# Gated two-branch decode attention: both A heads of a set scored by row on VectorE, one softmax merge per set, and a re-dealt indirect DMA

## The chip, the core and the metric

The kernel runs on one core of one Trainium2 chip. The metric is the device time of the program in microseconds (us), lower is better. Five engines matter: TensorE (PE, with its weight loads PEld), VectorE (DVE), ScalarE (ACT), GpSimd (POOL) and the sync queue (SP) that issues nearly all DMAs. "Span" is the time from the first to the last instruction in the profiled execution.

## The reference

Two attention blocks answer one query token (x, 448 numbers) from caches of 8192 keys, and a sigmoid gate mixes them. Block A has 16 heads with a cache of its own each; block B has 16 query heads that share 8 caches in pairs. Head size is 256, all in fp32.

```python
def _A_ref(x, k_cache, v_cache, wq, wo):          # H, Dh = 16, 256
    q = (x @ wq).reshape(B, Sq, H, Dh).transpose(0, 2, 1, 3)
    scores = jnp.einsum("bhqd,bhkd->bhqk", q, k_cache) * (Dh ** -0.5)
    p = _softmax(scores, axis=-1)
    o = jnp.einsum("bhqk,bhkd->bhqd", p, v_cache)
    return o.transpose(0, 2, 1, 3).reshape(B, Sq, H * Dh) @ wo
...                                               # _B_ref: the same, k and v repeated for pairs of heads
x = A_x
g = _sigmoid((x * gate_w).sum(-1, keepdims=True))
return g * a + (1 - g) * b
```

The key caches and the query weights of both blocks are multiplied by 64 when the inputs are made, so the softmax is sharp.

## The kernel before, in words

**The stream.** All inputs (caches, query weights `wq`, output weights `wo`) are laid out by the host in the order of use in one array, `stream`. SP copies it through a ring of three slots, each 128 partitions by 15872 floats; one DMA fills one slot but at the end, where the last slots come in several pieces. A slot's next DMA is issued when every instruction that reads the slot is done. `plan()` (L220) cuts the stream into these fills and nothing else sets the order of the work: the program walks through the fills, and the pieces in each, and issues for each piece what can be done with it (`piece`, L625).

**Sets and tiles.** The work goes in 8 sets. A set has one B cache (two query heads, unit 2), then two A heads (units 0 and 1; `UNITS`, L199, gives the order 2, 0, 1). A unit is cut into 4 tiles of 2048 keys: a K tile and a V tile of 4096 floats per partition each. V tiles follow their K tiles with a lead of three (`LEAD`): after K tile i comes V tile i-3. A set's `wo` comes in behind the fourth tile of the next set, and the next set's `wq` behind the eighth. I number K and V tiles 0 to 95 through the whole stream; set 7 has tiles 84 to 87 (B), 88 to 91 (first A head, A0) and 92 to 95 (second A head, A1).

**Two ways to score a K tile.** `scores` (L454) has the keys turned (256 numbers of a key down the partitions): PE multiplies them with the query in 8 matmuls into PSUM (`sc`), DVE takes the minimum of the negated scores (`mn`, `st`), ACT exponentiates (`px`), and DVE transposes the 128x512 result (`pr`) into weights for PE. `scores_by_row` (L481) has one key per row: DVE multiplies the whole tile in place by the query laid over all partitions (`slot<-slot,qa`, 4096 elements per partition), sums each key's 256 products (`sr<-slot`), takes the minimum over a partition and over 32 partitions (`mn`, `mt`, `st`), ACT exponentiates 16 numbers (`pxr`), and DVE spreads them over the columns that PE wants (`pr<-pxr,cols`). Where a tile is cut by the end of a slot, multiply and sum run once for each part. `BY_ROW` (L200) says which units go by row; before, that is unit 0 of each set (A0), and the host lays out the keys to suit.

**After the scores.** `attend` (L509) multiplies a V tile with `pr` on PE in 8 matmuls and accumulates in PSUM (`o`); after a unit's fourth V tile `take` (L521) folds the two halves (ACT, then DVE) into `ob`. Each tile has its own minimum and sum; `gather` (L529) puts them in `gs`, and `combine` (L543) merges them for one unit on one partition: a matmul with ones, a minimum (`mnr`), exponentials (`ew`, ACT), products and a sum (`es`, `z`), a reciprocal, and weights times the gate (`wr`). `column` (L567) turns these into a column (`sel`) by a matmul, `project_o` (L577) applies it to `ob`, and `emit_set`/`emit` multiply with `wo` into `Y`. These steps are put off by `wait` and `tick` (L615, L618): a tick comes at the end of every K tile, and of the last three V tiles. The order of instructions on each engine is the order in which the program issues them, and each engine takes its own in that order.

**Query and side DMA.** `project` makes a set's queries on PE from `wq`; `spread` (L436) lays them out for both ways of scoring. For set 4 part of `wq` comes by an indirect DMA that POOL issues, from an array `side` into the front of fill 23's slot, in a choice of partitions (`SIDE_SHARE`, L208) that gives some of the 16 DMA engines more rows than others; the rest (`ws`) comes in the stream.

**The end.** The last V tile comes in three pieces and set 7's `wo` in four; then `project_o` for the last unit, four `emit` calls, a copy of `Y` (`ys`) and the DMA out.

Of the kernel before, what the change touches and what calls it, by code (L numbers as in the profile page):

```python
# [10 lines left out]
P = 128  # L11
# [188 lines left out]
BY_ROW = {(s, 0) for s in range(NS)}  # L200
# [7 lines left out]
SIDE_SHARE = {0: 8, 2: 8, 7: 8, 8: 8, 15: 8, 4: 7, 1: 5, 3: 1, 6: 1, 10: 1}  # L208
# [3 lines left out]
SB, SA = 2 * DH, 64  # L212
# [54 lines left out]
def gated_decode_attention_kernel(  # L267
# [23 lines left out]
    zero = const.tile([P, P], BF16, name="zero")  # L291
    nc.vector.memset(zero, 0.0)

    POS, CAP = {}, {}
    for M in (2, 1):
        r = R[M]
        POS[M] = const.tile([P, NG, r], F32, name=f"pos{M}")
        nc.gpsimd.iota(POS[M], pattern=[[BLK + r, NG], [1, r]], base=0, channel_multiplier=-1,
                       allow_small_or_imprecise_dtypes=True)
        nc.vector.tensor_scalar(POS[M], POS[M], 0.0, None, op0=OP.is_equal)  # L300
        mask = const.tile([P, NT], F32, name=f"mask{M}")
        nc.vector.tensor_reduce(mask, POS[M].rearrange("p g (t m) -> p t g m", m=M), axis=AX.XY, op=OP.add)

        CAP[M] = const.tile([P, NT], F32, name=f"cap{M}")
        nc.vector.tensor_scalar(CAP[M], mask, 3.0e38, OFF, op0=OP.mult, op1=OP.add)
# [15 lines left out]
    rows4 = const.tile([P, 4], F32, name="rows4")  # L321
# [6 lines left out]
    in4 = const.tile([P, 2, NG], F32, name="in4")  # L328
    nc.vector.tensor_copy(in4[:, 0, :], rows4)
# [6 lines left out]
    cols = const.tile([P, NT, NG, NT], F32, name="cols")  # L336
    nc.vector.memset(cols, 0.0)
    for t in range(NT):
        nc.vector.tensor_copy(cols[:, t, :, t], in4[:, 1, :])

    spread32 = const.tile([2 * BLK, P], F32, name="spread32")
    nc.vector.memset(spread32, 0.0)
    nc.vector.memset(spread32[BLK:BLK + 1, :], 1.0)

    QB = {}
    for par in range(2):
        for r in (r for r in range(3) if (par, r) not in BY_ROW or (par + 2, r) not in BY_ROW):
            QB[par, r] = const.tile([P, 2, 64], F32, name=f"qb{par}{r}")
            nc.vector.memset(QB[par, r], 0.0)

    xz = const.tile([P, KF + 2, BLK], F32, name="xz")
    nc.vector.memset(xz, 0.0)
# [15 lines left out]
    gate = const.tile([1, 2], F32, name="gate")  # L370

    def clear(t, n):
        nc.tensor.matmul(t[:, :n], zero, zero[:, None, :n // 4].to_broadcast([P, 4, n // 4]), start=True, stop=False, skip_group_check=True)
# [10 lines left out]
    def prepare(gw):  # L384
        clear(YY[0], D)
        gp = ps_s.tile([1, 1], F32, name="sm")
        for c in range(KF + 1):
            nc.tensor.matmul(gp, xz[:, c, 0:1], gw[:, c:c + 1], start=(c == 0), stop=(c == KF))
# [3 lines left out]
        nc.vector.reciprocal(gate[:, 0:1], ge)  # L392
        nc.vector.tensor_scalar(gate[:, 1:2], gate[:, 0:1], -1.0, 1.0, op0=OP.mult, op1=OP.add)
# [5 lines left out]
    def project(s, c0, w):  # L399

        if c0 == 0:
            QR[s] = ps_s.tile([2 * BLK, 2 * DH], F32, name="sm")
        q = QR[s]
        for j in range(w.shape[1]):
            a, c = divmod(c0 + j, KF)
            for a in (a,) if a < 2 else (0, 1):
                c = c if c0 + j < 2 * KF else KF
                nc.tensor.matmul(q[BLK * a:BLK * (a + 1), :], xz[:, c if c < KF else KF + a, :], w[:, j, :],
                                 start=(c == 0), stop=(c == KF), skip_group_check=True)
        if c0 + w.shape[1] == 2 * KF + 1:  # L410
            copy_out(s, q)
# [5 lines left out]
    def project_side(s, view, far):  # L417
# [4 lines left out]
        for a in range(2):  # L422
            nc.tensor.matmul(q[BLK * a:BLK * (a + 1), :], xz[:, KF + a, :], rest, start=True, stop=False,
                             skip_group_check=True)
# [11 lines left out]
    def spread(s):  # L436
# [7 lines left out]
        for r, a, h, M in ((2, 0, 0, 2), (0, 1, 0, 1), (1, 1, 1, 1)):  # L444
            if (s, r) in BY_ROW:
                qa = ps_s.tile([P, DH], F32, name="sm")
                nc.tensor.matmul(qa, spread32, qr[:, h * DH:(h + 1) * DH], start=True, stop=True)
                QA[s, r] = small.tile([P, DH], F32, name="qa", bufs=1)
                nc.scalar.activation(QA[s, r], qa, AF.Copy, scale=-scale)
                continue  # L450
            nc.vector.tensor_scalar(QB[s % 2, r][:, :, BLK:BLK + M], qt[:, h:h + M, :, a].rearrange("p h e -> p e h"),
                                    -scale, None, op0=OP.mult)

    def scores(u, t, j0, kt):  # L454
# [6 lines left out]
        qb = QB[u[0] % 2, u[1]]  # L461
# [10 lines left out]
        nc.vector.tensor_tensor(st[:, 0, t:t + 1], mn, CAP[M][:, t:t + 1], op=OP.min)  # L472
        px = small.tile([P, NB * BLK], F32, name="px")
        nc.scalar.activation(px, sc, AF.Exp, bias=st[:, 0, t:t + 1], scale=-1.0, accum_out=st[:, 1, t:t + 1])
        pr = small.tile([P, NB * BLK], F32, name="pr", bufs=LEAD + 2)
# [5 lines left out]
    def scores_by_row(u, t, j0, kt):  # L481
# [10 lines left out]
        if j0 + n < ROWS:  # L492
# [9 lines left out]
        pr = small.tile([P, NB * BLK], F32, name="pr", bufs=LEAD + 2)[:, :ROWS * NG * NT].rearrange(  # L502
            "p (q c k) -> p q c k", c=NG * NT, k=2)
# [25 lines left out]
    def gather(u):  # L529

        M = heads(u)
        GS[u] = small.tile([P, 2, NG, NT, M], F32, name=f"gs{M}")
        st = ST[u][:, :, None, :].to_broadcast([P, 2, NG, NT])
        if u in BY_ROW:
            nc.vector.tensor_tensor(GS[u][:, :, :, :, 0], st, in4[:, :, :, None].to_broadcast([P, 2, NG, NT]), op=OP.mult)
        elif M == 1:
            nc.vector.tensor_tensor(GS[u][:, :, :, :, 0], st, POS[M][:, None].to_broadcast([P, 2, NG, NT]), op=OP.mult)
        else:
            pos = POS[M].rearrange("p g (t m) -> p g t m", m=M)
            for k in range(2):  # L540
                nc.vector.tensor_tensor(GS[u][:, k], ST[u][:, k, None, :, None].to_broadcast([P, NG, NT, M]), pos, op=OP.mult)

    def combine(u):  # L543

        M = heads(u)
        n = NG * NT
        gi = 1 if u[1] == 2 else 0
        T = ps_s.tile([1, 2, n * M], F32, name="sm")
        nc.tensor.matmul(T, ones, GS[u].rearrange("p k g t m -> p k (g t m)"), start=True, stop=True)
        mn = small.tile([1, 2], F32, name="mnr")  # L550
        z = small.tile([1, 2], F32, name="z")
        ew = small.tile([1, 2 * n], F32, name="ew")[:, :n * M]
        es = small.tile([1, 2 * n], F32, name="es")[:, :n * M]
        nc.vector.tensor_reduce(mn[:, :M], T[:, 0, :].rearrange("p (c m) -> p m c", m=M), axis=AX.X, op=OP.min)
        for m in range(M):
            nc.scalar.activation(ew[:, m::M], T[:, 0, m::M], AF.Exp, bias=mn[:, m:m + 1], scale=-1.0)
# [232 lines left out]
```

## Time and profile before

| what | value |
|---|---|
| time, median of 3 runs (lowest to highest) | 1005.79 us (1005.64 to 1006.03) |
| time of the profiled execution | 1005.72 us |
| its span | 1004.1 us |
| bytes moved, mean rate over the span | 432.51 MB, 431 GB/s |
| DMA queue of the stream, share of 16 engines' time | 99.3% |
| instructions on PE / PEld / DVE / ACT / POOL | 3176 / 3176 / 650 / 307 / 20 |
| ACT busy | 94.0 us (9%) |

All instructions carry the line of one helper that records them (L150), so groups are told apart by their tiles, written out<-in. A view by groups gives: engine, operation, tiles, shape, count, then busy us, mean ns of one, and the idle time before them. A view in order of time gives: start in us from the span's start, length, engine, what, count, and in brackets the idle time of the engine before it with what ended that. PE needs two MATMUL records for each matmul of fp32 data (16 records are one tile's 8 matmuls).

### The profile page before, as it was taken

Reading aid. Unit: us, or ns where it says so; the run is one execution under the profiler, and the core shown is the slowest. Engines: PE = TensorE matmul, PEld = TensorE weight load, DVE = VectorE, ACT = ScalarE, POOL = GpSimd, SP = SyncE. Lnnn points to the kernel's source line nnn. Section 1 sums busy time; section 2 is a strip of 40 time slices with the busy share of each in tenths; the row PEclk is TensorE's granted clock in tenths of the full one; section 3 lists DMA queues with packets and bytes.
Section 4 is the critical chain, followed back from the end, with each engine's and each line's share of the span. In section 5 each row is a group of like instructions: output and inputs, shape, how many; then the busy total and the mean of one; then the engine's idle time right before and its main releaser. Section 6 shows DMA issues by size and latency. Waiting matters only on the chain.

```text
span 1004.1 us, 7447 instructions
## 1 busy us (share of the span) xinstructions
PE 586.9 (58%) x3176; PEld 172.7 (17%) x3176; DVE 459.2 (46%) x650; ACT 94.0 (9%) x307; POOL 4.4 (0%) x20
## 2 busy tenths in 40 slices
PE   0845745565754655656837566445755646656466
PEld 0211211121211111112212121111211112111112
DVE  2386223961248521467213951248521585215852
ACT  0100110010100110001100011100110001100101
POOL 1000000000000000000000000000000000000000
PEclk9977777767777887777777777877777767977779
DMA  9999999999999999999999999999999999999998
GB/s 405 441 432 420 443 441 416 438 441 435 426 428 445 433 436 425 437 432 433 436 435 426 440 436 428 431 440 435 428 433 436 434 437 426 431 440 441 423 421 366
DMA packets 9257, 432.51 MB, mean 431 GB/s; under 512 B 1105, under 2 KB 1233, under 8 KB 1873
## 3 DMA queue, kind: packets, MB, share of 16 engines
q1 hardware_dynamic: 9080, 431.14, 99.3%
q0 software_dynamic: 144, 0.89, 0.2%
q8 instruction: 25, 0.41, 0.1%
q14 instruction: 8, 0.07, 0.0%
HBM read 433.20 MB, written 0.00 MB: 431 GB/s over the span
## 4 chain that ended last, share of the span: by engine, by line
DMA 71%; PE 14%; DVE 13%; ACT 1%; issue 0%; SPq 0%
DMA slot<-in_stream_dram 71%; PE o L150 7%; DVE sr L150 5%; DVE slot L150 5%; PE sc L150 5%; PE sm L150 2%; DVE pr L150 1%; DVE mn L150 1%; ACT px L150 1%; ACT pxr L150 0%; DVE st L150 0%; ACT ew L150 0%; DVE mt L150 0%; DVE ob L150 0%; DVE es L150 0%
## 5 line engine op out<-in xcount | busy, mean ns | idle before, releaser
L150 PE MATMUL o<-slot,pr 128*32 128x512 f32 (+1 forms) x1536 | 345.4, 756 | 206.7 <-DMA slot<-in_stream_dram 206.7
L150 PE MATMUL sc<-slot,qb 128*32 128x512 f32 x1024 | 195.3, 725 | 111.2 <-DMA slot<-in_stream_dram 111.0
L150 DVE TENSOR_REDUCE mn<-sc 128x1 f32<-128x512 f32 x64 | 44.2, 690 | 326.6 <-PE sc L150 291.2
L150 DVE TENSOR_TENSOR slot<-slot,qa 128x4096 f32<-128x4096 f32 (+6 forms) x39 | 142.4, 3652 | 45.0 <-DMA slot<-in_stream_dram 45.0
L150 PEld LDWEIGHTS o<-slot,pr 128*32 128x32 f32 (+1 forms) x1536 | 80.3, 143 | 385.7 <-DMA slot<-in_stream_dram 231.2
L150 DVE TENSOR_REDUCE sr<-slot 128x16 f32<-128x4096 f32 (+6 forms) x39 | 142.5, 3654 | 1.3
L150 PEld LDWEIGHTS sc<-slot,qb 128*32 128x32 f32 x1024 | 45.7, 130 | 227.5 <-DMA slot<-in_stream_dram 127.1
L150 ACT ACTIVATE px<-sc,st 128x512 f32<-128x512 f32 x64 | 44.0, 687 | 395.6 <-DVE st L150 395.6
L150 DVE STREAM_TRANSPOSE pr<-px 128x512 f32<-128x512 f32 x64 | 45.6, 713 | 54.1 <-ACT px L150 54.1
L150 PE MATMUL sm<-slot,xz 128*32 128x512 f32 (+2 forms) x130 | 46.2, 694 | 32.9 <-DVE xz L150 22.7
L150 ACT ACTIVATE pxr<-sr,st 128x16 f32<-128x16 f32 x32 | 9.8, 308 | 377.0 <-DVE st L150 377.0
L150 PE MATMUL sm<-sel,ob 128*128 128x1 f32 (+1 forms) x96 | 18.2, 294 | 33.9 <-DVE ob L150 33.9
L150 DVE SCALAR_TENSOR_TENSOR ob<-o,half,ob 128x256 f32<-128x256 f32 x24 | 11.4, 473 | 49.6 <-ACT ob L150 49.5
L150 PEld LDWEIGHTS sm<-sel,ob 128*128 128x128 f32 x96 | 16.2, 237 | 58.7 <-DVE ob L150 51.0
L150 PEld LDWEIGHTS sm<-slot,xz 128*32 128x32 f32 (+1 forms) x130 | 11.3, 131 | 65.3 <-issue 29.7
L150 DVE TENSOR_TENSOR pr<-pxr,cols 128x256 f32<-128x256 f32 x32 | 13.6, 426 | 15.0 <-ACT pxr L150 15.0
L150 PE MATMUL Y<-slot,ocs 128*1 128x448 f32 (+1 forms) x176 | 17.0, 450 | 4.7 <-DMA slot<-in_stream_dram 4.6
L150 ACT ACTIVATE ob<-o,half 128x256 f32<-128x256 f32 x24 | 11.3, 469 | 47.4 <-PE o L150 47.2
L150 PE MATMUL sm<-px,spread 64*128 64x256 f32 x16 | 7.6, 568 | 13.1 <-DVE es L150 13.1
L150 PE MATMUL sm<-ones,wr 1*128 1x1 f32 x48 | 9.9, 273 | 8.3 <-DVE wr L150 8.2
L150 PEld LDWEIGHTS sm<-ones,wr 1*128 1x128 f32 x48 | 7.8, 203 | 30.4 <-DVE wr L150 15.5
L150 ACT ACTIVATION_READ_ACCUMULATOR px<-sc,st 128x1 f32 x64 | 12.3, 193 | 0.0
(69 smaller groups left out, 150.0 us busy)
## 6 DMA issues: line engine op xcount, KB each, us to landing
slot<-in_stream_dram SPq DMA_DIRECT2D x47, 7936.0 KB, 41.9
slot<-in_stream_dram SPq DMA_DIRECT2D x1, 7944.0 KB, 21.7
slot<-in_stream_dram SPq DMA_DIRECT2D x1, 7840.0 KB, 46.8
slot<-in_stream_dram SPq DMA_DIRECT2D x1, 7776.0 KB, 48.6
slot<-in_stream_dram SPq DMA_DIRECT2D x1, 5792.0 KB, 42.2
slot<-in_stream_dram SPq DMA_DIRECT2D x1, 5376.0 KB, 34.9
slot<-in_stream_dram SPq DMA_DIRECT2D x2, 2048.0 KB, 33.4
slot<-in_stream_dram SPq DMA_DIRECT2D x1, 2816.0 KB, 31.1
```

The source lines that it names most:

```text
L150: ins = getattr(engine, method)(*args, **kw)
```

## The change

It has six parts.

1. `BY_ROW` now holds units 0 and 1 of every set: A1 is scored by row too. `in_order` lays out its keys to suit. `spread` makes one 128x512 tile `qa` for both A heads (one matmul, one ACT copy) where it made one of 128x256 for A0 and a scaled copy `qb` for A1. `pr` of the A tiles becomes a tile of its own, `prr`, with 8 buffers; the B tiles' `pr` has 4.
2. `combine` and `column` run once for a set, after the last K tile of A1, for all four heads: `gather` puts all in one `gs`; the products go on DVE (B) and ACT (A). `project_o` of the set's first two units moves behind that `column`.
3. The indirect DMA goes into 64 partitions (before 55) with 6 pieces of 704 floats each (before 7 of 576); `ws` has 1472 floats per partition (before 1856). The fills of the stream are the same but for that one piece.
4. The two matmuls of the last `wq` piece become one of 64 columns.
5. The gate is a DVE product, a DVE sum and one matmul, where it was four matmuls; `gate` has four entries.
6. Constants: the masks for one head alone and `spread32` go, zeroed tiles are joined in one (`empty`), `zero` shrinks, `ys` uses a scratch buffer.

The core of the diff:

```diff
-BY_ROW = {(s, 0) for s in range(NS)}
+BY_ROW = {(s, r) for s in range(NS) for r in (0, 1)}
...
-SIDE_SHARE = {0: 8, 2: 8, 7: 8, 8: 8, 15: 8, 4: 7, 1: 5, 3: 1, 6: 1, 10: 1}
+SIDE_SHARE = {0: 8, 2: 8, 7: 8, 8: 8, 15: 8, 4: 6, 1: 5, 5: 3, 13: 3, 14: 3, 6: 2, 10: 1, 3: 1}
...
-SB, SA = 2 * DH, 64
+SB, SA = 2 * DH, 192
...
     def spread(s):
...
-        for r, a, h, M in ((2, 0, 0, 2), (0, 1, 0, 1), (1, 1, 1, 1)):
-            if (s, r) in BY_ROW:
-                qa = ps_s.tile([P, DH], F32, name="sm")
-                nc.tensor.matmul(qa, spread32, qr[:, h * DH:(h + 1) * DH], start=True, stop=True)
-                QA[s, r] = small.tile([P, DH], F32, name="qa", bufs=1)
-                nc.scalar.activation(QA[s, r], qa, AF.Copy, scale=-scale)
-                continue
-            nc.vector.tensor_scalar(QB[s % 2, r][:, :, BLK:BLK + M], qt[:, h:h + M, :, a].rearrange("p h e -> p e h"),
-                                    -scale, None, op0=OP.mult)
+        nc.vector.tensor_scalar(QB[s % 2][:, :, BLK:BLK + 2], qt[:, :, :, 0].rearrange("p h e -> p e h"),
+                                -scale, None, op0=OP.mult)
+        qa = ps_s.tile([P, 2 * DH], F32, name="sm")
+        nc.tensor.matmul(qa, rows4[:2 * BLK, 1:2].to_broadcast([2 * BLK, P]), qr, start=True, stop=True)
+        both = small.tile([P, 2 * DH], F32, name="qa")
+        nc.scalar.activation(both, qa, AF.Copy, scale=-scale)
+        for r in range(2):
+            QA[s, r] = both[:, r * DH:(r + 1) * DH]
...
-    def combine(u):
...
-        for m in range(M):
-            nc.scalar.activation(ew[:, m::M], T[:, 0, m::M], AF.Exp, bias=mn[:, m:m + 1], scale=-1.0)
...
+    def combine(s):
...
+        nc.vector.tensor_reduce(mn, T[:, 0], axis=AX.X, op=OP.min)
+        nc.vector.tensor_tensor(ew, T[:, 0], mn[:, :, None].to_broadcast([1, NG, n]), op=OP.subtract)
+        nc.scalar.activation(ew, ew, AF.Exp, scale=-1.0)
+        nc.vector.tensor_tensor(es, ew, T[:, 1], op=OP.mult)
+        nc.vector.tensor_reduce(z, es, axis=AX.X, op=OP.add)
+        nc.vector.reciprocal(z, z)
+        nc.vector.tensor_tensor(z, z, gate, op=OP.mult)
...
+        for h in range(NG):
+            if h < 2:
...
+                nc.vector.tensor_scalar(w, ew[:, None, h, :, None].to_broadcast([1, 2, n, 2]), z[:, h:h + 1], None,
+                                        op0=OP.mult)
+            else:
...
+                nc.scalar.activation(w, ew[:, None, h, :, None].to_broadcast([1, NG, n, 2]), AF.Copy, scale=z[:, h:h + 1])
...
             if t == NT - 1:
                 gather(u)
-                wait(1, combine, u)
-                wait(2, column, u)
+                if u[1] == UNITS[-1]:
+                    s = u[0]
+                    wait(1, combine, s)
+                    wait(2, column, s)
+                    for r in UNITS[:2]:
+                        wait(2 if s == NS - 1 else 3, project_o, (s, r))
...
-                    if u != TILES[-1][0]:
+                    if u[1] == UNITS[-1] and u[0] < NS - 1:
                         wait(1, project_o, u)
```

**DVE at the last K tile (tile 95).** `sc` is the scores in PSUM, `slot_50` and `slot_51` two slots of the ring, `sr` the row sums. Before:

```order
L150 TENSOR_REDUCE mn_84<-sc 128x1
L150 TENSOR_TENSOR st_82<-mn_84,cap_11_59 128x1
L150 STREAM_TRANSPOSE pr_85<-px_61 128x8x2x32
L150 TENSOR_TENSOR gs_81_121<-st_82,pos_9_57 128x32
L150 TENSOR_REDUCE mnr_99<-sm 1x1
```

Now, at the same place:

```order
L150 TENSOR_TENSOR slot_50<-slot_50,qa_68 128x2560
L150 TENSOR_REDUCE sr_84<-slot_50 128x10
L150 TENSOR_TENSOR slot_51<-slot_51,qa_68 128x1536
L150 TENSOR_REDUCE sr_84<-slot_51 128x6
L150 TENSOR_REDUCE mn_77<-sr_84 128x1
L150 STREAM_TRANSPOSE mt_86<-mn_77 128x32
L150 TENSOR_REDUCE st_75<-mt_86 128x1
L150 TENSOR_TENSOR prr_96<-pxr_88,empty_63 128x256
L150 TENSOR_TENSOR gs_82<-st_75,in_13_61 128x2x16
L150 TENSOR_REDUCE mnr_102<-sm 1x4
```

Three small instructions per tile are replaced by a multiply and a sum over the whole tile, in two parts here, and four small ones.

**PE at the end of the stream.** `o<-slot` are the matmuls of V tiles 92 to 95, `sm<-gs` is combine's matmul, `sm<-ones,wr` (now `sm<-ones,px`) column's, `sm<-sel,ob` project_o's. Before:

```order
L150 MATMUL sm<-sel_110,ob_114 128x1 x2
L150 MATMUL o<-slot_51,pr_87 32x512 x8
L150 MATMUL o<-slot_51,pr_88 32x512 x8
L150 MATMUL sm<-gs_81_121,ones_49 1x32
L150 MATMUL o<-slot_51,pr_89 32x512 x8
L150 MATMUL sm<-ones_49,wr_109 128x1
L150 MATMUL o<-slot_52,pr_85 32x512 x8
L150 MATMUL sm<-sel_111,ob_115 128x1 x2
```

Now:

```order
L150 MATMUL o<-slot_51,prr_93 32x512 x8
L150 MATMUL o<-slot_51,prr_94 32x512 x8
L150 MATMUL sm<-gs_82,ones_49 1x128
L150 MATMUL o<-slot_51,prr_95 32x512 x8
L150 MATMUL sm<-ones_49,px_58 128x1 x3
L150 MATMUL sm<-sel_108,ob_98 128x2 x2
L150 MATMUL sm<-sel_108,ob_99 128x1 x2
L150 MATMUL o<-slot_52,prr_96 32x512 x8
L150 MATMUL sm<-sel_108,ob_100 128x1 x2
```

combine's and column's matmuls keep their places among the V tiles; the project_o of the set's first two units (`ob_98`, `ob_99`) now stands between column and the last V tile's matmuls.

More of the change, by code (lines that the diff above doesn't have):

```diff
@@ L567, in column @@
[L567 to L575 removed]
+        T = ps_s.tile([1, 2, NG, n], F32, name="sm")
+        nc.tensor.matmul(T, ones, GS.pop(s).rearrange("p k h g t -> p (k h g t)"), start=True, stop=True)
```

150 lines of the change are left out of this document (65 added, 85 removed).

## The prediction

> **What bounds the kernel now.** First the page: the engines' busy time, the slices, and the issues.
>
> ```profile
> PE 586.9 (58%) x3176; PEld 172.7 (17%) x3176; DVE 459.2 (46%) x650; ACT 94.0 (9%) x307; POOL 4.4 (0%) x20
> ...
> DMA  9999999999999999999999999999999999999998
> ...
> slot<-in_stream_dram SPq DMA_DIRECT2D x47, 7936.0 KB, 41.9
> ```
>
> The DMA engines are busy in every slice; DVE in less than half of the span. A fill lands 41.9 us after its issue (median), and moving it takes 7936 KB / 431 GB/s = 18.9 us, so fills are queued some 23 us ahead. The stream sets the time as long as slots come free early enough and little is left to do when the last byte lands. The chain that ended last, in order of time, shows how little that is before:
>
> ```profile
> 965.10 35.92 DMA slot<-in_stream_dram
> 1001.06 0.99 PE Y L150 x32
> 1002.07 0.28 DVE ys L150
> ```
>
> All of the last 36 us is waiting for the stream; behind it come the last output matmuls, a copy and the DMA out. The change puts no byte less into the stream worth naming, so the questions are two: does DVE still free the slots in time, and when is it done with the last K tile?
>
> **What a K tile costs DVE, by either way.** The groups of instructions, shapes apart:
>
> ```profile
> L150 DVE TENSOR_REDUCE sr<-slot 128x16 f32<-128x4096 f32 x25 | 110.5, 4420 | 0.9
> L150 DVE TENSOR_TENSOR slot<-slot,qa 128x4096 f32<-128x4096 f32 x25 | 110.4, 4418 | 26.6 <-DMA slot<-in_stream_dram 26.6
> L150 DVE STREAM_TRANSPOSE pr<-px 128x512 f32<-128x512 f32 x64 | 45.6, 713 | 54.1 <-ACT px L150 54.1
> L150 DVE TENSOR_REDUCE mn<-sc 128x1 f32<-128x512 f32 x64 | 44.2, 690 | 326.6 <-PE sc L150 291.2 <-PE sm L150 35.3
> ```
>
> By row it is 4.42 + 4.42 us and small steps; by PE's scores 0.69 + 0.71 and small steps. The four A0 tiles of set 7 and one A1 tile, in DVE's order of time:
>
> ```profile
> 919.69 4.43 DVE L150 TENSOR_TENSOR slot<-slot,qa 128x4096 f32<-128x4096 f32 x1 [8.60 <-DMA slot<-in_stream_dram]
> ...
> 942.51 4.42 DVE L150 TENSOR_TENSOR slot<-slot,qa 128x4096 f32<-128x4096 f32 x1
> 946.96 4.42 DVE L150 TENSOR_REDUCE sr<-slot 128x16 f32<-128x4096 f32 x1
> ...
> 952.88 0.48 DVE L150 SCALAR_TENSOR_TENSOR ob<-o,half,ob 128x256 f32<-128x256 f32 x1
> 953.28 3.88 DVE L150 TENSOR_TENSOR slot<-slot,qa 128x3584 f32<-128x3584 f32 x1
> ...
> 963.88 0.18 DVE L150 TENSOR_TENSOR gs<-st,in 128x32 f32<-128x32 f32 x1
> 963.98 0.69 DVE L150 TENSOR_REDUCE mn<-sc 128x1 f32<-128x512 f32 x1
> ...
> 979.61 0.69 DVE L150 TENSOR_REDUCE mn<-sc 128x1 f32<-128x512 f32 x1 [9.31 <-PE sc L150]
> ...
> 981.34 0.71 DVE L150 STREAM_TRANSPOSE pr<-px 128x512 f32<-128x512 f32 x1 [0.84 <-ACT px L150]
> ```
>
> A whole tile by row takes DVE from 942.51 to 952.88, 10.37 us; one that is cut takes from 953.28 to 963.88, 10.60; `ob` adds 0.40 and `gs` 0.10. A tile by PE's scores takes it from 979.61 to 982.05, 2.4, with a wait for ACT in it. DVE is not idle between these tiles: the first waited for its fill, and all later ones for DVE itself.
>
> **The stream's pace, and whether slots come free.** PE's rows at 938.42, 957.19 and 975.90 show when fills 49, 50 and the second part of 51 landed:
>
> ```profile
> 938.42 9.20 PE L150 MATMUL o<-slot,pr 128*64 128x512 f32 x32 [5.88 <-DMA slot<-in_stream_dram]
> 953.42 1.01 PE L150 MATMUL sm<-sel,ob 128*128 128x2 f32 x4 [5.80 <-DVE ob L150]
> 957.19 3.64 PE L150 MATMUL o<-slot,pr 128*32 128x512 f32 x16 [2.76 <-DMA slot<-in_stream_dram]
> 975.90 1.08 PE L150 MATMUL sc<-slot,qb 128*32 128x512 f32 x4 [5.92 <-DMA slot<-in_stream_dram]
> ```
>
> A fill of 15872 floats per partition each 18.7 us, so one K and one V tile (8192 floats) each 9.7 us: less than the 10.4 us that DVE needs. Eight by-row tiles take DVE 8 x 10.4 = 83 us; the stream needs 8 x 9.7 = 77.3 us for them and twice 4.2 us for the 3584 floats of `wo` and of `wq` that lie between, 85.8 in all. So within a set DVE falls back by some us at a time, not without end, and in the four B tiles (39 us of stream, 2.4 us of DVE each) it catches up. A fill holds at most some 2 by-row tiles, 21 us of DVE; 2 us more than a fill's 18.7; with up to 5 us carried over from the fills before, a slot is free at most about 26 us after it landed. Its next DMA is due when the two fills behind it have landed, 37.4 us after: over 10 us remain. I count nothing for slots. If the cover went, each us beyond it would be a us of idle DMA, seven times over (rival 1).
>
> **The last set, step by step.** Fill 48 brings tiles 88 and 89, and DVE starts at 919.69, as before: by the argument above it has caught up, and the fill's contents and place are unchanged. From here to the end DVE has eight by-row tiles in a row and always more landed than it can eat: five whole (88, 89, 90, 92, 94), three cut by a slot's end (91, 93, 95), two `ob`, one `gs` between. 5 x 10.37 + 3 x 10.60 + 2 x 0.40 + 0.10 = 84.55 us, so the last `gs` starts at 919.69 + 84.55 = 1004.24 and ends at 1004.4. **That is about 18 us later than before**, and later than the stream's end, as these rows of all engines show (`gs` for the last unit at 986.05):
>
> ```profile
> 986.05 0.15 DVE L150 TENSOR_TENSOR gs<-st,pos 128x32 f32<-128x32 f32 x1
> 987.48 1.92 PE L150 MATMUL o<-slot,pr 128*32 128x512 f32 x16 [1.44 <-DMA slot<-in_stream_dram]
> ...
> 989.22 0.22 PE L150 MATMUL sm<-gs,ones 128*1 128x32 f32 x2
> ...
> 989.48 0.16 DVE L150 TENSOR_REDUCE mnr<-sm 1x1 f32<-1x16 f32 x1 [3.29 <-PE sm L150]
> ...
> 990.54 0.33 DVE L150 TENSOR_SCALAR wr<-ew,rz,gate 1x128 f32<-1x128 f32 x1
> ...
> 994.18 0.38 PE L150 MATMUL sm<-ones,wr 1*128 1x1 f32 x2
> 994.60 0.17 ACT L150 ACTIVATE sel<-sm 128x1 f32<-128x1 f32 x1 [4.65 <-PE sm L150]
> ...
> 997.29 1.05 PE L150 MATMUL o<-slot,pr 128*32 128x512 f32 x4 [0.25 <-DMA slot<-in_stream_dram]
> ...
> 999.44 0.63 PE L150 MATMUL sm<-sel,ob 128*128 128x1 f32 x4 [1.09 <-DVE ob L150]
> ...
> 1001.06 0.68 PEld L150 LDWEIGHTS Y<-slot,ocs 128*1 128x1 f32 x32 [0.34 <-DMA slot<-in_stream_dram]
> ```
>
> Before, combine, column and project_o went between the landings of V tiles 93 to 95 and cost nothing. Now PE has done V tiles 92 and 93 long since and sits in its order at combine's matmul, with V tile 94, column, two project_o and V tile 95 queued behind it. What follows `gs` lies open:
>
> - combine's matmul and the handover to `mnr`: 989.48 - 989.22 = 0.26 at full clock; I take 0.5: 1004.9.
> - the chain from `mnr` to the end of `wr` took 989.48 to 990.87, 1.39 us; now a subtraction, a product with the gate and a second `wr` on DVE come in (0.2 + 0.2 + 0.33), and rows are two to four times as wide: 2.3 us, to 1007.2. ACT's two copies run beside it.
> - V tile 94 runs meanwhile, 8 matmuls, 1.92 us when PE is warm; but PE has stood idle since V tile 93, some 15 us, and behind 2.8 us of idleness the row at 957.19 took 3.64 us for the same 16 records. I take 3.64: 1008.3, so PE and not `wr` is late.
> - column: 0.42 us for one (994.18 to 994.60), three with 0.2 for each further: 0.8, to 1009.1; `sel` 0.25; two project_o at 0.63: 1010.6.
> - V tile 95: 1.92, to 1012.6.
> - from there it is the old end: V's last matmul ended at 997.29 + 1.05 = 998.34, the span at 1004.1, and 0.34 of that was a wait for the stream that is gone: 5.4 us, to **1018.0**.
>
> The execution's own time is 1005.72 us for a span of 1004.1, 1.6 us around it, and it stands within 0.1 us of the median shown. Prediction: 1018.0 + 1.6 = **1019.6 us**, 1.4% slower.
>
> **PE's clock, a place to weigh.** The granted clock in three stretches:
>
> ```profile
> 970.00:975.90 5.90, 0.00 (x0) 0.79 0.98 423
> 975.90:979.30 3.40, 3.40 (x16) 0.50 1.00 431
> 987.40:989.40 2.00, 1.93 (x18) 1.00 1.03 442
> ```
>
> Columns: stretch, length, PE busy, clock, DMA share, GB/s. Behind 5.9 us without a matmul PE gets half its clock for 3.4 us. [...] With all of the tail at half clock V tile 95 takes 3.64 and the project_o 1.0 each (the row at 953.42), 2.5 us more (1022.1 us of time); with PE at full clock throughout V tile 94 ends before `wr` does, and the sum is 1.1 us less (1018.5).
>
> **What else the change touches.** PE loses the `sc` matmuls of 32 A1 tiles, DVE their 32 x (0.69 + 0.71) us, and the set-wise combine saves small instructions on DVE and ACT. All of it lay beside the stream and buys nothing, and DVE's small work is replaced by some six times as much. The side DMA moves 64 rows of 16.9 KB for 55 of 16.1 KB, 0.19 MB more, and `ws` is 0.20 MB smaller: no sum changes. How evenly the 16 engines end can change: a row is 0.6 us of one engine (431/16 = 27 GB/s), and the smaller `ws` saves each engine 384 x 4 B x 8 partitions = 12.3 KB, 0.45 us. Three new rows are then 1.4 us later for an engine; one row less (engine 4) is 0.9 earlier. The last landing is hidden under DVE's lateness; only the landing of fill 48 counts, -0.9 to +1.4 us, and I take 0. Set-up (gate, masks, queries) lies before the first fill's landing or in set 0, which is not near the end: 0.
>
> **Rivals.** *1. Slots run out.* If DVE's lateness holds up PE as well (PE takes its queue in order, and the query matmuls of the next set wait for an ACT copy that stands behind `pxr`), a slot might come free more than 37.4 - 2 us after landing. Price: from that point each set loses what is above, say 3 us at each of seven boundaries, 21 us: 1040. For it: margins of 10 us, worked out from means. Against: eight tiles fit into the stream's 85.8 us, and PE is busy for only 3.6 of each 9.7 us. Chance 0.07. *2. No change, or faster.* The mechanism would be that DVE is done with tile 95 when V tile 95's last piece lands, near 997: then the old end stands, and the lighter PE and the re-dealt rows may give back up to 0.9 us (1004.8 to 1006). For this a by-row tile must take (997 - 1.6 - 919.69) / 8 = 9.5 us instead of 10.4 (1.6 for two `ob`, `gs` and three cuts); that is the point from which it decides. Multiply and sum alone are 8.84, and the small steps with the wait for `pxr` 1.5, alike in all rows; I see nothing that shrinks them. Chance 0.04. *3. The change doesn't do what it says*: A1 still scored from PSUM; the program's order shows the by-row rows at tile 95, so 0.
>
> **How the numbers follow.** The forecast has 0.89. Its own range: DVE's sum is firm to 0.5 us, fill 48's landing -0.9 to +1.4, the tail -1.1 to +2.5 by the clock and 1 us for handovers: 1016.5 to 1024.0. I leave out both rivals, 0.11. Below some 0.2% (2 us) a measurement of this kernel can't be told from no change. Slower by more 0.96, within 0.2% 0.03, faster by more 0.01.
>
> **What would show it.** Right: DVE's rows from 919.7 show eight by-row tiles at 10.4 us without a gap, the last `gs` near 1004; the chain's last 85 us are DVE; the DMA slices stay at 9 up to the last, which drops; the stream's last landing stays near 1001; `ys` near 1016. Wrong: DVE waiting for DMA inside set 7, a slice of DMA under 9 in mid-stream (rival 1), or `gs` before 997 (rival 2).

## The result, and the profile after

The changed kernel takes 1023.56 us (median of 6 runs, 1020.73 to 1025.23) and the kernel before 1005.79 us (6 runs, 1005.61 to 1006.03): a ratio of 1.0174, 95% interval 1.0163 to 1.0185, so 1.7% slower. The prediction was 1019.6 us in a range of 1016.5 to 1024.0. The profiled execution of the changed kernel took 1020.73 us with a span of 1019.1 us. It is the shortest of the six, so its tail is the best case; a second profile comes with the experiments.

From the page of the changed kernel: the engines, the slices, the chain that ended last by engine, and the issues of whole fills.

```profile
PE 531.1 (52%) x2606; PEld 154.6 (15%) x2606; DVE 711.9 (70%) x680; ACT 81.7 (8%) x291; POOL 4.2 (0%) x19
...
DMA  9999999999999999999999999999999999999992
...
DMA 56%; DVE 33%; PE 9%; ACT 2%; issue 1%; SPq 0%
...
slot<-in_stream_dram SPq DMA_DIRECT2D x47, 7936.0 KB, 40.0
```

The slices say where the time is not: the DMA engines work at 9 tenths through 39 of 40 slices, as before, so the stream was never held up. Only the last slice fell, from 8 to 2. The 250 us that DVE gained stand beside the stream everywhere but at the end. Fills land 40.0 us after their issue, 41.9 before, so they queue some 2 us shorter. The chain's DVE share went from 13% to 33%.

In DVE's order of time, set 7: the first two starts of by-row tiles, then the last `gs` and what follows it (columns as before: start, length, what, idle time ahead of it and its releaser).

```profile
920.65 4.43 DVE L150 TENSOR_TENSOR slot<-slot,qa 128x4096 f32<-128x4096 f32 x1 [5.36 <-DMA slot<-in_stream_dram]
...
931.01 4.42 DVE L150 TENSOR_TENSOR slot<-slot,qa 128x4096 f32<-128x4096 f32 x1
...
1005.18 0.19 DVE L150 TENSOR_TENSOR gs<-st,in 128x32 f32<-128x32 f32 x1
1006.04 0.21 DVE L150 TENSOR_REDUCE mnr<-sm 1x4 f32<-1x64 f32 x1 [0.68 <-PE sm L150]
...
1007.69 0.53 DVE L150 TENSOR_SCALAR px<-ew,z 1x64 f32<-1x64 f32 x2
...
1017.08 0.28 DVE L150 COPY px<-Y 128x112 f32<-128x112 f32 x1 [2.44 <-PE Y L150]
```

Eight tiles fill DVE from 920.65 to 1005.18 with no wait for a DMA in between: 84.53 us. The copy of `Y` is at 1017.08, where it stood at 1002.07 before.

PE's order of time over the same tail:

```profile
1005.42 0.37 PE L150 MATMUL sm<-gs,ones 128*1 128x128 f32 x1 [13.46 <-DVE gs L150]
...
1005.80 3.62 PE L150 MATMUL o<-slot,prr 128*32 128x512 f32 x13
1009.35 0.95 PE L150 MATMUL sm<-ones,px 1*128 1x1 f32 x6
1010.63 1.10 PE L150 MATMUL sm<-sel,ob 128*128 128x2 f32 x8 [0.33 <-DVE sel L150]
1011.66 1.92 PE L150 MATMUL o<-slot,prr 128*32 128x512 f32 x16
1014.70 0.63 PE L150 MATMUL sm<-sel,ob 128*128 128x1 f32 x4 [1.11 <-DVE ob L150]
1015.26 1.75 PE L150 MATMUL Y<-slot,ocs 128*1 128x112 f32 x64
```

PE waited 13.46 us for `gs`, and then everything behind it in its queue, V tiles 94 and 95 with it, runs one after the other.

### The profile page after: what moved, and what is told of

Its sections match the earlier page's. It is cut to its first block, busy times and chain, and to the rows that moved or that the text cites. A ratio compares the mean times of both kernels' runs of the same rounds, so it can differ in the third digit from the quotient of the medians.

```text
span 1019.1 us, 6340 instructions
## 1 busy us (share of the span) xinstructions
PE 531.1 (52%) x2606; PEld 154.6 (15%) x2606; DVE 711.9 (70%) x680; ACT 81.7 (8%) x291; POOL 4.2 (0%) x19
## 4 chain that ended last, share of the span: by engine, by line
DMA 56%; DVE 33%; PE 9%; ACT 2%; issue 1%; SPq 0%
DMA slot<-in_stream_dram 56%; DVE sr L150 14%; DVE slot L150 14%; PE o L150 4%; PE sc L150 2%; PE sm L150 2%; DVE prr L150 1%; ACT pxr L150 1%; DVE mn L150 1%; DVE mt L150 1%; DVE st L150 1%; DVE ob L150 1%; ACT px L150 0%; DVE pr L150 0%; PE Y L150 0%
## 5 line engine op out<-in xcount | busy, mean ns | idle before, releaser
L150 DVE TENSOR_TENSOR slot<-slot,qa 128x4096 f32<-128x4096 f32 (+7 forms) x80 | 285.3, 3566 | 55.5 <-DMA slot<-in_stream_dram 55.5
L150 PE MATMUL o<-slot,prr 128*32 128x512 f32 x1024 | 197.1, 857 | 187.8 <-DMA slot<-in_stream_dram 187.8
L150 DVE TENSOR_REDUCE sr<-slot 128x16 f32<-128x4096 f32 (+7 forms) x80 | 285.3, 3567 | 2.7
L150 PE MATMUL o<-slot,pr 128*64 128x512 f32 x512 | 150.3, 728 | 120.0 <-DMA slot<-in_stream_dram 120.0
L150 PE MATMUL sc<-slot,empty 128*32 128x512 f32 x512 | 98.9, 762 | 76.1 <-DMA slot<-in_stream_dram 76.0
L150 PEld LDWEIGHTS o<-slot,prr 128*32 128x32 f32 x1024 | 41.5, 142 | 310.5 <-DMA slot<-in_stream_dram 217.6
L150 PEld LDWEIGHTS o<-slot,pr 128*64 128x64 f32 x512 | 42.1, 166 | 219.5 <-DMA slot<-in_stream_dram 132.6
L150 PE MATMUL sm<-slot,empty 128*32 128x512 f32 (+2 forms) x106 | 44.9, 704 | 42.5 <-DVE empty L150 22.8
L150 DVE TENSOR_TENSOR prr<-pxr,empty 128x256 f32<-128x256 f32 x64 | 27.2, 425 | 29.9 <-ACT pxr L150 29.9
L150 PEld LDWEIGHTS sc<-slot,empty 128*32 128x32 f32 x512 | 24.0, 136 | 136.1 <-DMA slot<-in_stream_dram 84.1
```

The source lines that it names most:

```text
L150: ins = getattr(engine, method)(*args, **kw)
```

## The experiments

The theory is that of the prediction: set 7's second A head by row makes DVE 18 us late, and PE's order puts the whole tail behind that. Its rivals are that the slots run short in mid-stream, that the re-dealt indirect DMA or the set-wide merge costs the time, and, for the 4.0 us between forecast and median, that a fill lands later or that PE's clock is lower in the tail. Each run was compared with runs of the kernel before on the same chip. The second run with zeros and the first run with set 7's second A head back on PE, both below, were on another chip than the rest; the kernel before took 1005.88 us there, and 1005.79 to 1006.09 on the first.

### The changed kernel once more

No edit; a second profile and more times.

> The changed kernel once more, for a second profile, since its six times lie 4.5 us apart (1020.7 to 1025.2) where those of before lie 0.4 apart, and the profiled execution was the fastest. Theory (the end hangs on DVE's eight by-row tiles behind the landing of fill 48): 1020 to 1025 us again, eight tiles of 10.4 us without a gap, and what differs from the first profile is the start of the first tile (fill 48's landing) by up to 4 us. Rival: the start is alike within 1 us and the difference lies in the tail behind the last gs (PE's clock), up to 3 us.

Measured: 1023.11 us (4 runs, 1022.77 to 1024.42), ratio 1.0176 (1.0159 to 1.0193), span 1021.1 us. PE's tail in this execution:

```profile
1011.30 2.56 PE L150 MATMUL o<-slot,prr 128*32 128x512 f32 x16
1014.95 1.01 PE L150 MATMUL sm<-sel,ob 128*128 128x1 f32 x4 [1.09 <-DVE ob L150]
1015.89 3.17 PE L150 MATMUL Y<-slot,ocs 128*1 128x112 f32 x64
```

The last `gs` and the copy of `Y` on DVE:

```profile
1004.96 0.18 DVE L150 TENSOR_TENSOR gs<-st,in 128x32 f32<-128x32 f32 x1
...
1019.13 0.28 DVE L150 COPY px<-Y 128x112 f32<-128x112 f32 x1 [4.23 <-PE Y L150]
```

DVE's first tile starts at 920.44 and the last `gs` at 1004.96, both 0.2 us earlier than in the first profile, and still the span is 2.0 us longer. V tile 95 takes 2.56 us instead of 1.92, project_o 1.01 instead of 0.63, the output matmuls 3.17 instead of 1.75: 0.64 + 0.38 + 1.42 = 2.44 us, and that is the 2.0 us and the 0.2 with a little over. The same instructions in the same order run at another clock: over 1012 to 1016 it was 1.00 in the first profile and 0.56 in the second. So the expectation that fill 48's landing sets the two apart fell, and its rival, the tail's clock, held.

### The kernel before, with only set 7's second A head by row

```diff
-BY_ROW = {(s, 0) for s in range(NS)}
+BY_ROW = {(s, 0) for s in range(NS)} | {(NS - 1, 1)}
...
```

The rest of the edit gives `qa` a second buffer, since two heads need one.

> The kernel before with one unit more by row: A1 of set 7 alone. Theory: the whole loss comes from the last set, so this alone gives it, about 1021 us (1018 to 1025): DVE's last gs near 1007, since the merge of each unit now stands between the tiles. Rival 1, by-row tiles cost something in every set: an eighth of 17.8 us, 1008. Rival 2, the set-wise merge and its place in PE's queue are the loss: at most 1010, since this kernel has the old merge.

Measured: 1021.62 us (4 runs, 1020.85 to 1022.25), ratio 1.0158 (1.0141 to 1.0175). As the theory had it, one of the eight units that the change moves to DVE gives 15.8 us, nine tenths of the whole loss. In DVE's order of time:

```profile
930.22 0.17 DVE L150 TENSOR_REDUCE mnr<-sm 1x2 f32<-1x32 f32 x1
...
1007.79 0.18 DVE L150 TENSOR_TENSOR gs<-st,in 128x32 f32<-128x32 f32 x1
...
1017.22 0.27 DVE L150 COPY ys<-Y 128x112 f32<-128x112 f32 x1 [2.44 <-PE Y L150]
```

The last `gs` is 2.6 us later than in the changed kernel although DVE's first tile starts 0.8 us earlier (919.85 against 920.65), so DVE's full stretch is 3.4 us longer, since here the softmax steps of the units before it (such as the one from 930.22 on) stand on DVE between the by-row tiles, where DVE has no time to spare. The tail behind it, 9.43 us to the copy, is 2.5 us shorter than the 11.90 of the changed kernel's first profile, where the wider merge and two more `project_o` (1.10 us) stand. So one softmax step for a set moves work out of DVE's full stretch into the open tail. How the 1.9 us between this run's median and the changed kernel's divides between that and the tail's clock was not tested.

### The kernel before, with the second A head by row in all sets but the last

```diff
-BY_ROW = {(s, 0) for s in range(NS)}
+BY_ROW = {(s, 0) for s in range(NS)} | {(s, 1) for s in range(NS - 1)}
...
```

The rest of the edit gives `qa` three buffers.

> The kernel before with A1 by row in sets 0 to 6, and set 7 as it was. Theory: slots have room, so 1005.5 to 1006.5 us, although DVE's busy time goes from 459 to some 680 us. Rival 1 (slots run out, or DVE's work costs in every set): seven eighths of the loss, 1021.

Measured: 1006.39 us (10 runs, 1006.20 to 1006.97), ratio 1.0005 (0.9995 to 1.0014). The page's slices and the end of its chain:

```profile
DMA  9999999999999999999999999999999999999998
...
965.78 35.98 DMA slot<-in_stream_dram
1001.80 0.99 PE Y L150 x32
```

Seven more units by row, DVE busy for 689.5 us instead of 459.2, and the chain ends as it did before. The slots have the room that the prediction counted on; its first rival falls.

### The changed kernel, with set 7's units in the order A0, A1, B

```diff
-TILES = [((s, r), t) for s in range(NS) for r in UNITS for t in range(NT)]
+ORDER = [UNITS] * (NS - 1) + [[0, 1, 2]]
+TILES = [((s, r), t) for s in range(NS) for r in ORDER[s] for t in range(NT)]
...
```

The rest of the edit uses `ORDER` wherever the program or the host's layout went by `UNITS`.

> The changed kernel with set 7 in the order A0, A1, B, all else alike: as many by-row tiles and the same merge, but the four B tiles, 2.4 us of DVE each, come last. Theory: DVE catches up in them, 1006 to 1008 us. Rival 1 (a cost in every set) and the re-dealt indirect DMA as a rival: 1020 or more. Rival 2 (the merge behind the last K tile and its place in PE's queue): 1010 to 1014, as the merge still stands at the end.

Measured: 1011.1 us (4 runs, 1009.31 to 1011.72), ratio 1.0046 (1.0029 to 1.0063): 12.5 us of the loss go, and the expected 1006 to 1008 was missed. DVE's last `gs`, and PE from there:

```profile
986.93 0.25 DVE L150 TENSOR_TENSOR gs<-st,pos 128x32 f32<-128x32 f32 x2
```

```profile
996.45 0.82 PE L150 MATMUL sm<-ones,px 1*128 1x1 f32 x6
997.80 1.10 PE L150 MATMUL sm<-sel,ob 128*128 128x1 f32 x8 [0.53 <-ACT sel L150]
998.83 5.35 PE L150 MATMUL o<-slot,pr 128*64 128x512 f32 x16
```

With eight by-row tiles ahead of the four B tiles DVE catches up, and `gs` is back at 987. What is left is PE's queue: the last V tile waits behind column and project_o until 998.83 and then takes 5.35 us, part of it at a lower clock (0.70 over 1000 to 1004).

### The changed kernel, with the re-dealt indirect DMA alone, and without it

One run adds these two lines to the kernel before, the other takes them back in the changed kernel:

```diff
-SIDE_SHARE = {0: 8, 2: 8, 7: 8, 8: 8, 15: 8, 4: 7, 1: 5, 3: 1, 6: 1, 10: 1}
+SIDE_SHARE = {0: 8, 2: 8, 7: 8, 8: 8, 15: 8, 4: 6, 1: 5, 5: 3, 13: 3, 14: 3, 6: 2, 10: 1, 3: 1}
...
-SB, SA = 2 * DH, 64
+SB, SA = 2 * DH, 192
```

> The kernel before with the re-dealt indirect DMA alone (64 partitions, 6 pieces, ws of 1472 floats). Theory: this kernel ends with the stream, whose bytes are the same; three engines get 1.4 us more and the others 0.2 to 0.9 less, so the last landing moves by +0.4 to +1.2 us: 1006.2 to 1007.0. Rival (the deal is better balanced by itself): 1005.2 to 1005.6.

> The changed kernel with the indirect DMA dealt as before. Theory: fill 48 lands within 1.5 us of 919.7 and DVE's eight tiles take 84.5 us from there as ever, so the time stays at 1020 to 1025 us. Rival (the re-dealing is a part of the loss that matters): 1015 or less.

Measured: alone 1006.75 us (11 runs, 1006.42 to 1007.36), ratio 1.0007 (0.9998 to 1.0016); taken back 1023.36 us (4 runs, 1020.05 to 1024.87), ratio 1.0177 (1.0161 to 1.0193), the changed kernel's own 1.0174 to 1.0176. Where DVE sets the end the deal does nothing that can be seen. Where the stream sets it, 0.9 us were measured, inside the 1006.2 to 1007.0 expected, but the interval reaches below 1, so a cost is not shown.

### The changed kernel, with part of set 7's multiplications left out

```diff
-        nc.vector.tensor_tensor(kt, kt, QA[u][:, None, :].to_broadcast([P, n, DH]), op=OP.mult)
+        m = n // 2 if u == (NS - 1, 1) else n
+        nc.vector.tensor_tensor(kt[:, :m], kt[:, :m], QA[u][:, None, :].to_broadcast([P, m, DH]), op=OP.mult)
```

> The changed kernel with half of the multiply left out in the four A1 tiles of set 7 (the scores of half the keys of those tiles are then sums of the keys alone): 4 x 2.2 = 8.8 us of DVE less, in the last set only. Theory: the last gs comes 8.8 us earlier, near 996.4, and the time falls by as much, to some 1014.6 us (1011 to 1017). Rival (something else than DVE's work in set 7 sets the end, such as the merge's chain or PE): less than 3 us of it is seen.

Measured: 1012.33 us (4 runs, 1010.90 to 1014.38), ratio 1.0058 (1.0042 to 1.0074). DVE, one of the shortened tiles and the last `gs`:

```profile
962.73 2.28 DVE L150 TENSOR_TENSOR slot<-slot,qa 128x2048 f32<-128x2048 f32 x1
...
996.53 0.18 DVE L150 TENSOR_TENSOR gs<-st,in 128x32 f32<-128x32 f32 x1
...
1010.70 0.28 DVE L150 COPY px<-Y 128x112 f32<-128x112 f32 x1 [4.23 <-PE Y L150]
```

The kernel leaves out the multiplication for half of the keys in each of these four tiles, so their scores are sums of the keys alone; the instructions are otherwise the same. PE's tail ran here at the durations of the changed kernel's second profile (the wait for `Y` is 4.23 us in both), so the two can be set side by side: `gs` starts at 996.53 instead of 1004.96 and the copy at 1010.70 instead of 1019.13, 8.43 us earlier both. DVE's time in set 7 is passed on to the end in full. The median falls by more, 11.2 us; the 2.7 us beyond are within the 3.5 us that this run's four times are apart, and no profile says what they are.

### The changed kernel, with matmuls of zeros to keep PE's clock up

The first run puts 48 matmuls of 512 columns of zeros in bf16 between V tile 93 and combine; the second 60 there, 3 ahead of column and 5 ahead of the last project_o, as in these lines. Their product is not used.

```diff
+                if i >= len(TILES) - LEAD:
+                    idle({93: 60, 94: 3, 95: 5}[i])
...
```

> The changed kernel with 48 more matmuls (zeros, into a PSUM bank that nothing reads any more) in PE's queue between V tile 93 and combine's matmul, some 12 us in which PE otherwise stands idle. Theory: DVE's last gs stays at 1005.0 to 1005.3, and what differs between the runs of the changed kernel is the clock that PE is granted behind it; kept busy, PE ends the tail in some 12.8 us instead of 13.7 to 18: median near 1019.7 us with runs less than 1.5 us apart. Rival (the runs differ in where the stream or DVE stands): median and spread as before, 1023 and 3 to 4 us.

> The changed kernel with PE kept busy to the very last tile and in the tail: 60 matmuls of zeros (before 48, which ended 2.4 us before the last gs) between V tile 93 and combine's matmul, 3 before column and 5 before the last project_o, all into a PSUM bank that nothing reads. Theory (the clock granted in the tail makes the runs differ): PE at full clock from combine's matmul to the end; from the last gs to the copy of Y some 10.4 us, where the profiles so far show 11.9, 14.2 and 15.6; median near 1019 us and runs within 1.5 us. Rival (PE's clock isn't it): 1023 us and 3 to 4 us between runs again. If the clock falls all the same, nothing is told apart, and the profile's clock will show that.

Measured: the first 1023.7 us (5 runs, 1021.33 to 1025.28), ratio 1.0171 (1.0155 to 1.0188), no gain; the second 1019.34 us (4 runs, 1018.72 to 1019.87), ratio 1.0131 (1.0115 to 1.0146). Four stretches of the tail in the first (stretch, length, busy us and count of PE, PEld, DVE, ACT and POOL, granted clock, DMA share, GB/s):

```profile
1000.00:1004.00 4.00, 2.25 (x11) 0.80 (x9) 3.47 (x5) 0.36 (x2) 0.00 (x0) 1.00 0.11 43
1004.00:1008.00 4.00, 3.34 (x20) 1.30 (x21) 2.17 (x10) 0.99 (x4) 0.00 (x0) 0.72 0.00 0
1008.00:1012.00 4.00, 3.67 (x20) 2.91 (x23) 0.23 (x1) 0.52 (x3) 0.00 (x0) 0.50 0.00 0
1012.00:1016.00 4.00, 2.88 (x17) 0.49 (x9) 0.48 (x1) 0.47 (x1) 0.00 (x0) 0.50 0.00 0
```

and three of them in the second:

```profile
1004.00:1008.00 4.00, 3.61 (x27) 1.76 (x27) 1.98 (x10) 0.95 (x3) 0.00 (x0) 1.00 0.00 0
1008.00:1012.00 4.00, 3.60 (x24) 1.57 (x26) 0.23 (x1) 0.55 (x4) 0.00 (x0) 0.81 0.00 0
1012.00:1016.00 4.00, 3.74 (x72) 2.61 (x71) 0.48 (x1) 0.62 (x2) 0.00 (x0) 0.76 0.02 4
```

In the first the zeros ran out at 1002.25, PE stood idle for 2.41 us, and the clock fell when the tail had begun and stayed down to the end (0.50 over 1016 to 1020 too), though PE was busy for most of each stretch; the 1019.7 us expected were missed. In the second the gap ahead of combine is 0.57 us and the clock holds for longer, but it falls too. From the last `gs` to the copy of `Y` 10.4 us were expected and 12.07 were measured, no less than the 11.90 of the changed kernel's first profile. So the 4.2 us by which its median lies under the changed kernel's are not the clock's alone: in this profile the last `gs` starts at 1004.15, 0.8 to 1.0 us ahead of the changed kernel's two.

What the clock can cost is better read where DVE stands in the same place. The last `gs` starts at 1004.45 in the run with the old deal and at 1004.42 in the first run with zeros. Their copies of `Y`, in this order:

```profile
1016.41 0.28 DVE L150 COPY px<-Y 128x112 f32<-128x112 f32 x1 [2.44 <-PE Y L150]
```

```profile
1020.06 0.27 DVE L150 COPY px<-Y 128x112 f32<-128x112 f32 x1 [4.23 <-PE Y L150]
```

They are 3.65 us apart, with V tile 95 at 1.92 and 3.64 us and the output matmuls at 1.75 and 3.17. The clock was 0.87 over 1008 to 1012 and 1.00 over 1012 to 1016 with the old deal, 0.50 over both with the zeros. So PE's clock behind `gs` is worth up to 3.65 us in these profiles; in the changed kernel's median execution, which was not profiled, I estimate it at some 3 us, since 1023.56 lies 2.8 us over the execution of its first profile and 3.5 over that of the run with the old deal, both with the short tail. Whether holding the clock narrows the spread is not shown: the second run's four times lie 1.2 us apart, but the changed kernel's second set of four only 1.7. Nor is it told apart whether the smaller gap or the zeros within the tail made the second run faster.

### The changed kernel, with set 7's second A head back on PE, and then with V tile 95 ahead of the merge

```diff
-BY_ROW = {(s, r) for s in range(NS) for r in (0, 1)}
+BY_ROW = {(s, r) for s in range(NS) for r in (0, 1)} - {(NS - 1, 1)}
...
```

The rest of the edit brings back the constants and the query tile that scoring one A head on PE needs, and `prr` has 7 buffers.

The second run has this edit too, and takes set 7's column and first two project_o behind V tile 95 in PE's queue. The third is the second with the old deal of the indirect DMA.

```diff
-                    wait(2, column, s)
+                    wait(3 if s == NS - 1 else 2, column, s)
                     for r in UNITS[:2]:
-                        wait(2 if s == NS - 1 else 3, project_o, (s, r))
+                        wait(3, project_o, (s, r))
```

> The changed kernel with A1 of set 7 alone scored by PE, as before; by row in sets 0 to 6, the set-wise merge, the re-dealt DMA and all else stay (prr has 7 buffers for 8, for room). Theory: the loss is DVE's work in set 7, and the merge between V tiles 94 and 95 costs at most 1 to 2 us at PE, so 1006 to 1008 us. Rival (the merge and its place in PE's queue cost several us of their own, as the 1011.1 of the kernel with B last could mean): 1010 to 1012.

> The changed kernel with set 7's A1 scores back on TensorE, and now also with set 7's column matmuls and its first two project_o behind V tile 95 in TensorE's queue instead of ahead of it. Theory (what is left of the loss, 3.4 us at 1009.3, is V95 standing behind the merged step, and the halved clock that falls on it there): V95 starts with its last piece near 997.5 instead of 998.7 and takes about 2 us instead of 3.64, so 1006 to 1007.5. Rival (the set-wide softmax step and the merged products cost the 3.4 us by themselves, wherever they stand): stays at 1008.5 to 1009.5.

> The same with the indirect DMA dealt as before. Theory (the new deal costs 0.5 to 0.9 us wherever the DMA engines set the end, as they do again here): 0.5 to 0.9 us under the run beside it, 1005.5 to 1006.8, level with the kernel before and not under it by more than 0.2%. Rival (the deal does nothing): the same time as the run beside it.

Measured: the first 1009.28 us (6 runs, 1008.01 to 1011.20), ratio 1.0031 (1.0019 to 1.0043); the second 1007.4 us (11 runs, 1006.47 to 1009.17), ratio 1.0016 (1.0007 to 1.0025); the third 1007.37 us (11 runs, 1006.49 to 1008.19), ratio 1.0012 (1.0003 to 1.0021). PE's end in the first:

```profile
995.13 1.44 PE L150 MATMUL sm<-ones,px 1*128 1x1 f32 x6
996.90 1.86 PE L150 MATMUL sm<-sel,ob 128*128 128x2 f32 x8 [0.33 <-DVE sel L150]
998.69 3.64 PE L150 MATMUL o<-slot,pr 128*32 128x512 f32 x16
```

and in the second:

```profile
997.14 1.05 PE L150 MATMUL o<-slot,pr 128*32 128x512 f32 x4 [0.24 <-DMA slot<-in_stream_dram]
998.12 0.82 PE L150 MATMUL sm<-ones,px 1*128 1x1 f32 x6
999.43 1.57 PE L150 MATMUL sm<-sel,ob 128*128 128x2 f32 x12 [0.48 <-DVE sel L150]
1000.93 2.67 PE L150 MATMUL Y<-slot,ocs 128*1 128x112 f32 x64
```

The first takes 14 us of the loss away and missed its 1006 to 1008: V tile 95 starts only at 998.69, after column and project_o, and runs at half clock (0.50 over 996 to 1004). (The profiled execution, 1011.20 us, is the slowest of its six.) In the second V tile 95 is taken piece by piece as it lands and is done at 998.19, and the time is 1.9 us lower, 1.5 by the ratios; the two ratios' intervals still overlap. The third was expected 0.5 to 0.9 us under the second and is level with it, so that expectation fell. What is left to the kernel before, 1.3 us by the medians and 1.6 by the two profiles, lies behind V tile 95: column, one `sel`, three project_o, and the output matmuls, which start at 1000.93 instead of 1000.00 and take 2.67 us instead of 2.01. None of these is faster than the kernel before.

## Why the prediction was right, and what was mis-sized

- **What bounds the kernel, and the slots.** Right. The slices stay at 9 up to the last, and seven more by-row units away from the end cost 0.6 us, which can't be told from nothing.
- **A by-row tile, and DVE's sum.** Right: 84.55 us were forecast for set 7's eight tiles, 84.53 were measured. That this is the cause is shown from both sides: it alone in the kernel before gives 15.8 us, without it the changed kernel is 14 us faster, and 8.43 us less of it end the tail 8.43 us earlier.
- **Fill 48.** DVE started on it 0.96 us later in this execution than in the profile of before, within the bounds given, and it was taken as 0. Over the five profiles with the old deal the start lies within 919.69 to 919.96, over the eight with the new one and set 7 in the old order within 919.60 to 920.65, four of them beyond 920.4: the new deal seems to make it late in some executions, by some 0.6 us, which the times are too wide to confirm.
- **The tail's order.** Right: PE had waited 13.46 us at combine's matmul, V tile 94 ran at half clock (0.50 over 1004 to 1008) and was done 4.2 us after the start of `gs` (4.1 forecast), PE and not `px` was late, V tile 95 stood behind column and project_o. In the first profile the tail, from the start of the last `gs` to the end of the span, is 13.9 us against 13.8 forecast.
- **The tail's clock.** This is the mis-sized term. The sum had V tile 94 alone at half clock and V tile 95, the last project_o and the output matmuls at full. In the second profile these cost 2.4 us more, in the first run with zeros V tile 95 took 3.64. The bound of +2.5 us for a tail all at half clock was too small as well: it left out the last project_o (0.63 to 1.01) and the output matmuls (1.75 to 3.17), 1.8 us together, and a wider column. Its reading of the clock in the kernel before was short too: behind the 5.9 us without a matmul the half clock lasts beyond the 3.4 us of the row at 975.90, to 980.26, 4.4 us after the matmuls set in (0.50 over 979.30 to 980.00, 0.87 over 980 to 981). The median of 1023.56 lies 4.0 over the forecast, near the range's end, and two of the six executions lie beyond it; that the median is inside is luck in part, as the clock's share of the range was too small. That the second run with zeros comes to 1019.34, 0.3 us from the forecast, is luck: its tail holds matmuls that the forecast has not, and V tile 95 takes 2.56 us in it.
- **The merge and the smaller parts** were costed at nothing but for their place in the tail. Away from set 7 that holds: with the merge and the by-row tiles in every other set the time is 1007.4 us, and what it has over the kernel before lies behind V tile 95. Within set 7 the merge saves some 3.4 us of DVE's time and lengthens the tail by some 2.5, and even with DVE in time it holds up V tile 95.

## What to carry to other kernels

Work moved onto an idle engine was free here only where the stream still had something to bring (0.6 us for seven units); in the last stretch what of it was not done when the stream ended, and all that was queued in order behind it, was added to the end (15.8 us for one). So ask for each part of a uniform change what it does to the last tiles, and keep the old way there. And when a tail is summed on PE, price it at both clocks, every matmul of it, since one tail here, which began after a wait of 2.41 us, ran at 0.50 from 1006 to its end.

## What the runs showed of the hardware

Of two idle stretches of PE near the stream's end it was the shorter that the clock fell behind. Two stretches of the kernel before, in the first of which PE takes up work again:

```profile
992.00:993.00 1.00, 0.67 (x8) 0.29 (x12) 0.00 (x0) 0.00 (x0) 0.00 (x0) 1.00 0.98 418
993.00:994.00 1.00, 1.00 (x12) 0.13 (x4) 0.00 (x0) 0.00 (x0) 0.00 (x0) 1.00 0.97 410
```

and the same two in the changed kernel with set 7's second A head on PE:

```profile
992.00:993.00 1.00, 0.54 (x8) 0.24 (x12) 0.00 (x0) 0.08 (x1) 0.00 (x0) 1.00 1.01 426
993.00:994.00 1.00, 1.00 (x12) 0.18 (x8) 0.00 (x0) 0.00 (x0) 0.00 (x0) 0.72 0.98 406
```

Before, the clock stayed at 1.00 behind 2.89 us without a matmul; here it fell behind 2.76 us, and only when PE had been busy again for a us (0.98). In the second profile of the changed kernel it rises and falls again:

```profile
1009.00:1010.00 1.00, 0.94 (x7) 0.74 (x6) 0.02 (x1) 0.00 (x0) 0.00 (x0) 0.98 0.08 16
...
1012.00:1013.00 1.00, 1.00 (x12) 0.13 (x4) 0.00 (x0) 0.00 (x0) 0.00 (x0) 0.72 0.00 0
```

and in the first it rises and stays:

```profile
1009.00:1010.00 1.00, 1.00 (x9) 0.65 (x5) 0.00 (x0) 0.00 (x0) 0.00 (x0) 0.68 0.06 16
...
1012.00:1013.00 1.00, 1.00 (x16) 0.26 (x8) 0.00 (x0) 0.00 (x0) 0.00 (x0) 1.00 0.00 0
```

In the second profile the clock is 0.50 just ahead of the first stretch and just behind the other, and 1.00 in between. So a mean of 0.98 puts the rise at 1009.04, and 0.72 the fall at 1012.44: 3.40 us apart. The changes of the clock in the kernel before, worked out in the same way from rows of half a us, are at 932.48, 942.72, 952.96, 963.20, 973.44 and 980.26: 10.24 us apart, three steps of 3.41, and 6.82 at the end, two of them. The step of 3.41 is my estimate from these rows.

With the second A head on PE the clock fell at 993.44, and in the 3.41 us ahead of that PE had 0.98 us of matmuls. In the kernel before it stayed at 1.00 at 993.91, four steps behind 980.26, with 1.58 us of matmuls in the 3.41 us ahead. So it fell in the one although PE had not been idle throughout; why it stayed up in the other is not shown.

In the first run with zeros the clock fell at 1005.72 (a mean of 0.86 over 1005 to 1006) and stood at 0.50 from 1006 to 1020, some 14 us with V tiles, column, project_o and output matmuls in turn, PE busy for 3.67, 2.88 and 4.00 us of the three stretches of 4 us from 1008 on. In the changed kernel's two profiles the 3.41 us behind the rise hold column's end, the project_o and the start of V tile 95, and PE stands idle for 0.33 us of them in each. In the first profile, where the clock stayed at 1.00, 1.4 us of V tile 95 lie in them, and in the second, where it fell, 1.1 us. V tile 95 took 1.92 us in the first and in the run with the old deal, 2.56 us in the second and in the run with part of the multiplications left out. Whether where V tile 95 starts behind the rise is what set the two profiles apart is not shown: no run tried it by itself.
